# Attention, MLP and routed experts on one core: hidden values kept in PSUM, maxima scaled on ScalarE, sums applied to the attention's output in two of four batches

## Chip, cores and metric

One core of one Trainium2 chip. The metric is the time of one execution in microseconds of the device. Engines: PE is TensorE (matmul), PEld its weight loads, DVE is VectorE, ACT is ScalarE, POOL is GpSimd, SP is SyncE, which issues most DMAs here.

## What is computed

Attention with two kinds of masks, an MLP with a PReLU, and a layer of eight experts of which each token uses one.

```
scores = q @ k.T / 8;  masked (heads 0-3: local, 32 back; heads 4-7: every 32nd)
attn   = exp(scores - max);  attn /= sum + 1e-9;  a = attn @ v     # 4 batches, 8 heads, 576 x 64
h = x @ w_in;  g = max(h, 0) + alpha * min(h, 0);  y = g @ w_out   # 2304 x 512, 2048 hidden
e = argmax(y @ w_gate);  out = gate * sigmoid * relu(y @ w1[e]) @ w2[e]   # 8 experts, 1024 hidden
```

## The kernel before

The program fixes the order of the instructions on each engine by hand; an engine runs its instructions in that order, and waits where an input or a buffer is not there yet.

The attention works on groups: a pair of heads of one batch and one or two tiles of query rows (96, 126 or 72 rows), so two or four score tiles. There are 24 groups in batches 0 and 1 (`b < PE_MASK`) and 24 in batches 2 and 3. A group passes through a chain of steps, a step later each time: scores on TensorE (L218 to L240), in batches 0 and 1 with the mask added by a matmul; maxima on VectorE (L252), and L255 that multiplies them by the scale; the exponentials with their sums on ScalarE (L280); the sums' reciprocal on VectorE (L294, L295) and the normalization of the probabilities on GpSimd (L296; group 9 on VectorE); two steps after the scores their transposition on TensorE (L312) and a copy out of PSUM on ScalarE (L314); three steps after them the product with the values on TensorE (L327), a rounded copy on ScalarE (L366) and what rounding left out on VectorE (L371). The two parts are the input of the MLP.

The MLP runs over 6 blocks of 384 tokens with 16 iterations of 128 hidden values each, n = 0 to 95. Iteration n issues the first product of n + 2 (`mlp_in`, L438 to L440) into one of two PSUM banks, its activation (`mlp_act`: two relus on ScalarE, L447 and L448, and their sum on VectorE, L449), its split into a rounded part (L458 on ScalarE) and a rest (L460: GpSimd in block 0, VectorE later), and the second product of n (`mlp_out`, L473 to L475). Block 0 also carries a step of the attention in nearly every iteration, and up to iteration 11 the decoding of one weight: float64 words become two float32r parts by L401 (ScalarE), L405, L406 and L412 (VectorE), L420 (ScalarE) and L421 (GpSimd).

The order in an iteration: exponentials and reciprocals of the last step's group; first product of n + 2; values and output (L366, L371) of the group three steps back; the activation of n + 2; L420 and L421 of weight n + 4; scores and maxima of this step's group; L405, L406 and L412 of weight n + 5; second product of n with the transposition in between; L401 of weight n + 6; the split of n + 2.

Before block 0 stands a prologue of 13 steps for groups 0 to 9 with the decoding of the first weights. Steps 10 to 22 run in iterations 1 to 13 of block 0, eight more steps in each of the blocks 1 and 2, the others in block 3. The routing and the experts follow.

Of the kernel before, what the change touches and what calls it, by code (L numbers as in the profile page):

```python
# [15 lines left out]
P = 128  # L16
# [11 lines left out]
BLK = 384  # L28
# [21 lines left out]
# Splits ahead of the turn of the tokens of the place after next, by the kinds of three places in a row.  # L50
# [3 lines left out]
# When the parts of the second plan, its lists and its indices come: (place, position).  # L54
WHEN = ((0, 7), (1, 1), (1, 1), (1, 4), (1, 6))
OHP = 12
# Groups that VectorE normalizes, and groups whose scores come after matmuls that keep TensorE awake.
NRV = (9,)
FS = {2: 2}
# Parts of the first two products of the MLP that run between the last steps of the first attention.  # L60
# [23 lines left out]
def attention_prelu_mlp_routed_experts_kernel(  # L84
# [40 lines left out]
    with tc.manual_schedule():  # L125
# [20 lines left out]
        # A visit is a pair of heads of a batch and the groups of its rows that are worked on in turn.  # L146
# [56 lines left out]
        sc_t, p_t, pt_t, px_t = {}, {}, {}, {}  # L203
# [38 lines left out]
        def att_max(gi):  # L242
# [7 lines left out]
            if b < PE_MASK:  # L250
# [4 lines left out]
                nc.vector.tensor_scalar_mul(nm[:r, :nu], nm[:r, :nu], SCALE)  # L255
# [15 lines left out]
        def att_exp(gi):  # L271
# [5 lines left out]
            sm = apool.tile([P, 4], F32, tag="sm", name="sm", bufs=3)  # L277
# [12 lines left out]
        def att_norm(gi):  # L290
# [4 lines left out]
            nc.vector.reciprocal(sm[:r, :nu], sm[:r, :nu])  # L295
            (nc.vector if gi in NRV else nc.gpsimd).tensor_tensor(  # L296
# [6 lines left out]
        def att_transpose(gi, tag):  # L303
            local, js, r, kk = shape_of(gi)
            nu = 2 * len(js)
            pt = p_t.pop(gi)[0]
# [10 lines left out]
        def att_values(gi, tag):  # L317
# [7 lines left out]
            for ii, j in enumerate(js):  # L325
                for h2 in range(2):
                    mm(  # L327
                        px[h2 * D : (h2 + 1) * D, ii * P : ii * P + r],
                        v[:kk, j, h2, :],
                        ptt[:kk, h2 * len(js) + ii, :r],  # L330
                        start=True,
                        stop=True,
                    )
            px_t[gi] = px

        def att_store(gi):
            b, pr, g = groups[gi]
            local, js, r, kk = shape_of(gi)
            pxu = px_t.pop(gi).rearrange("p (u k) -> p u k", k=P)
            moves = []  # L340
# [51 lines left out]
        # A weight comes as a float64, two words; it leaves as the sum of two float32r.  # L392
# [49 lines left out]
        def mlp_act(n):  # L442
            c = n % NC1
            ph = h_t.pop(n)
            a = xpool.tile([P, BLK], F32, tag="a", name="a", bufs=2)
            bn = xpool.tile([P, BLK], F32, tag="bn", name="bn", bufs=1)
            nc.scalar.activation(out=a, in_=ph[:, :BLK], func=AF.Relu)  # L447
            nc.scalar.activation(out=bn, in_=ph[:, :BLK], func=AF.Relu, scale=-1.0)  # L448
            nc.vector.scalar_tensor_tensor(  # L449
                out=a, in0=bn, scalar=nalpha[:, c : c + 1], in1=a, op0=ALU.mult, op1=ALU.add  # L450
            )
            h_t[n] = a

        def mlp_split(n):
            a = h_t.pop(n)
            gh = xpool.tile([P, BLK], F32R, tag="gh", name="gh", bufs=3)
            gl = xpool.tile([P, BLK], F32R, tag="gl", name="gl", bufs=2)
            nc.scalar.activation(out=gh, in_=a, func=AF.Copy)  # L458
            eng = nc.gpsimd if n < NC1 else nc.vector
            eng.tensor_tensor(out=gl, in0=a, in1=gh.bitcast(F32), op=ALU.subtract)  # L460
# [97 lines left out]
        def route_parts(blk):  # L558
            """One-hot choice, weight and place in its expert's list of each token of a block."""
# [76 lines left out]
        def plan_parts(early):  # L636
            """A column is a list of up to 128 tokens of one expert, a place's tokens one or two columns. The
            first EARLY columns hold pairs of full lists of the tokens before the last block. The others
            of each expert come in pairs from C_P on, a last odd one from C_S on; but a last one of FEW
            tokens or less has its column from C_Q on."""  # L640
# [851 lines left out]
```

## Time and profile before

| | |
|---|---|
| median of 3 runs | 835.61 us (835.5 to 835.98) |
| span of the profiled execution | 831.9 us |
| busy PE, PEld | 784.2 us (94%), 659.6 us (79%) |
| busy DVE, ACT, POOL | 478.4 us (58%), 427.3 us (51%), 244.5 us (29%) |
| mean granted TensorE clock | 0.980 of full speed |

The span runs from the first to the last instruction; what starts and ends the execution around it is in the run's time only. Busy time of VectorE and GpSimd holds the time in which an issued operation waits for the other engine. In a timeline a row is an instruction with its start, its duration and its engine; starts of consecutive instructions of one engine can lie closer than their durations.

### The profile page before, as it was taken

The page shows a single profiled execution, that of the slowest core. Times are in us where ns is not written, and L with a number is a line of the kernel's source. Part 1 is how long each engine was busy: PE and PEld are TensorE (multiplying, and loading weights), DVE is VectorE, ACT ScalarE, POOL GpSimd, SP SyncE. Part 2 cuts the span into 40 slices and gives each one's busy share as a digit, 9 for nine tenths or more (in the row PEclk, how much of TensorE's full clock was granted, in tenths as well). Part 3 has the DMA queues.
Part 4 walks back from the last instruction along what each step waited for, and adds up shares of the span by engine and source line. Part 5 has one row for each costly group of instructions (what it writes and reads, how often), then busy time and mean ns, then how long its engine had stood idle before and what let it go on. Part 6 is the DMA issues. An engine that isn't in the chain of part 4 may idle for free. (4 is left out here: it accounts for less than half of the span.)

```text
span 831.9 us, 13663 instructions
## 1 busy us (share of the span) xinstructions
PE 784.2 (94%) x5032; PEld 659.6 (79%) x5035; DVE 478.4 (58%) x988; ACT 427.3 (51%) x1033; POOL 244.5 (29%) x168
## 2 busy tenths in 40 slices
PE   7687878999999999999999999999989998999995
PEld 4475766788888888888799898889878876878884
DVE  5989999345534554556333424757595447854422
ACT  6756665454455444665433333356534656655542
POOL 2756655200000000110000000032483354546422
PEclk9998999999999999999999999999999999999998
DMA  9716511101200121011000100362224577777421
GB/s 342 298 43 244 190 33 45 44 22 56 84 18 1 47 86 64 1 45 39 1 1 1 39 0 1 149 244 103 77 77 147 194 258 255 285 288 267 161 90 38
DMA packets 22621, 91.04 MB, mean 109 GB/s; under 512 B 3082, under 2 KB 7312, under 8 KB 15376
## 3 DMA queue, kind: packets, MB, share of 16 engines
q1 hardware_dynamic: 18816, 78.52, 26.6%
q0 software_dynamic: 3728, 11.55, 3.9%
q8 instruction: 41, 0.67, 0.3%
q14 instruction: 36, 0.29, 0.1%
HBM read 105.78 MB, written 9.97 MB: 139 GB/s over the span
## 5 line engine op out<-in xcount | busy, mean ns | idle before, releaser
L449 DVE SCALAR_TENSOR_TENSOR a<-bn,nalpha,a 128x384 f32<-128x384 f32 x96 | 73.2, 763 | 116.4 <-ACT bn L448 116.0
L438 PE MATMUL h<-xh,w 128*128 128x384 f32 x384 | 130.4, 340 | 0.4 <-ACT bn L448 0.4
L440 PE MATMUL h<-xh,w 128*128 128x384 f32 x384 | 129.9, 338 | 0.0
L439 PE MATMUL h<-xl,w 128*128 128x384 f32 x384 | 129.7, 338 | 0.0
L296 POOL TENSOR_TENSOR p<-p,sm 96x512 f32<-96x512 f32 (+2 forms) x47 | 48.7, 1036 | 267.6 <-DVE sm L295 255.3
L473 PE MATMUL acc<-w,gh 128*128 128x512 f32 x288 | 126.9, 441 | 0.0
L888 DVE TENSOR_TENSOR wx<-raw,wx 128x1024 fp32r<-128x1024 f32 x72 | 97.1, 1392 | 46.6 <-ACT wx L886 46.3
L475 PE MATMUL acc<-w,gl 128*128 128x512 f32 x288 | 115.8, 402 | 0.3 <-POOL gl L460 0.3
L474 PE MATMUL acc<-w,gh 128*128 128x512 f32 x288 | 115.6, 401 | 0.0
L886 ACT ACTIVATE wx<-raw 128x1024 fp32r<-128x1024 f32 x96 | 94.6, 1056 | 7.3 <-DMA raw<-in_wexp_dram 7.3
L447 ACT ACTIVATE a<-h 128x384 f32<-128x384 f32 x96 | 47.1, 491 | 99.7 <-PE h L440 99.6
L1042 PE MATMUL acc<-wx,hh 128*128 128x512 f32 x304 | 96.8, 400 | 0.0
L888 POOL TENSOR_TENSOR wx<-raw,wx 128x1024 fp32r<-128x1024 f32 x24 | 63.1, 2629 | 89.1 <-ACT wx L886 88.9
L438 PEld LDWEIGHTS h<-xh,w 128*128 128x128 f32 x384 | 73.1, 190 | 5.1 <-ACT bn L448 0.8
L439 PEld LDWEIGHTS h<-xl,w 128*128 128x128 f32 x384 | 72.9, 190 | 4.0
L440 PEld LDWEIGHTS h<-xh,w 128*128 128x128 f32 x384 | 72.6, 189 | 0.0
L895 POOL DMA_INDIRECT xg<-rows,idx_in x23 | 29.4, 1278 | 145.7 <-DVE a L449 139.3
L458 ACT ACTIVATE gh<-a 128x384 fp32r<-128x384 f32 x96 | 49.9, 520 | 42.6 <-DVE a L449 42.5
L475 PEld LDWEIGHTS acc<-w,gl 128*128 128x128 f32 x288 | 55.5, 193 | 14.2 <-POOL gl L460 0.8
L1042 PEld LDWEIGHTS acc<-wx,hh 128*128 128x128 f32 x304 | 56.5, 191 | 11.1
L473 PEld LDWEIGHTS acc<-w,gh 128*128 128x128 f32 x288 | 55.2, 192 | 11.1 <-issue 0.8
L460 DVE TENSOR_TENSOR gl<-a,gh 128x384 fp32r<-128x384 f32 x80 | 44.5, 556 | 28.7 <-ACT gh L458 16.6
(260 smaller groups left out, 1573.7 us busy)
## 6 DMA issues: line engine op xcount, KB each, us to landing
raw<-in_wexp_dram SPq DMA_DIRECT2D x64, 1024.0 KB
raw<-in_wp_dram SPq DMA_DIRECT2D x16, 1024.0 KB
qk<-in_qkv_dram SPq DMA_DIRECT2D x10, 576.0 KB
rows<-stage SPq DMA_DIRECT2D x15, 256.5 KB
v<-in_qkv_dram SPq DMA_DIRECT2D x8, 320.0 KB
qk<-in_qkv_dram SPq DMA_DIRECT2D x4, 384.0 KB
v<-in_qkv_dram SPq DMA_DIRECT2D x6, 256.0 KB
qk<-in_qkv_dram SPq DMA_DIRECT2D x4, 224.0 KB
```

The source lines that it names most:

```text
L296: (nc.vector if gi in NRV else nc.gpsimd).tensor_tensor(out=pt[:r, :nu, :kk], in0=pt[:r, :nu, :kk], in1=sm[:r, :nu].unsqueeze(2).to_broadc ...
L438: mm(ph[:, :BLK], w_in(c, 0, k), xh[:, k, :], start=(k == 0), stop=False)
L439: mm(ph[:, :BLK], w_in(c, 0, k), xl[:, k, :], start=False, stop=False)
L440: mm(ph[:, :BLK], w_in(c, 1, k), xh[:, k, :], start=False, stop=(k == KD - 1))
L449: nc.vector.scalar_tensor_tensor(out=a, in0=bn, scalar=nalpha[:, c : c + 1], in1=a, op0=ALU.mult, op1=ALU.add)
L458: nc.scalar.activation(out=gh, in_=a, func=AF.Copy)
L473: mm(o, gh[:, t], w_out(c, 0), start=(c == 0), stop=False)
L474: mm(o, gh[:, t], w_out(c, 1), start=False, stop=False)
L475: mm(o, gl[:, t], w_out(c, 0), start=False, stop=(c == NC1 - 1))
L886: nc.scalar.activation(out=w[:, :1024], in_=raw, func=AF.Copy)
L888: eng.tensor_tensor(out=w[:, 1024:], in0=raw, in1=w[:, :1024].bitcast(F32), op=ALU.subtract)
L1042: mm(po[i], h[:, h0 : h0 + P], wk[:, w0 : w0 + 512], start=st, stop=sp)
```

## The change

The activation works in PSUM: the second relu writes back into the bank of the first product, L449's sum goes there too, and the split reads it from there; the rest L460 is computed on VectorE in all blocks. In batches 0 and 1 the maxima are scaled by ScalarE, ahead of the exponentials; the probabilities are not normalized, but TensorE spreads the reciprocal sums over 64 partitions (a product with the identity) beside the values, ScalarE copies them to SBUF, and VectorE multiplies the output by them in PSUM. `sm` has four buffers in place of three; no group is normalized on VectorE. Comments are left out of the new text.

```diff
-NRV = (9,)
+NRV = ()
...
@@ att_max
-                nc.vector.tensor_scalar_mul(nm[:r, :nu], nm[:r, :nu], SCALE)
@@ att_exp
-            sm = apool.tile([P, 4], F32, tag="sm", name="sm", bufs=3)
+            sm = apool.tile([P, 4], F32, tag="sm", name="sm", bufs=4)
+            if b < PE_MASK:
+                nc.scalar.activation(out=nm[:r, : 2 * nj], in_=nm[:r, : 2 * nj], func=AF.Copy, scale=SCALE)
@@ att_norm
+            if groups[gi][0] < PE_MASK:
+                return
             (nc.vector if gi in NRV else nc.gpsimd).tensor_tensor(
@@ att_transpose
-            pt = p_t.pop(gi)[0]
+            pt, rs_t[gi] = p_t.pop(gi)
@@ att_values
+            rs = rs_t.pop(gi)
+            if b < PE_MASK:
+
+                for ii in range(len(js)):
+                    for h2 in range(2):
+                        u = h2 * len(js) + ii
+                        mm(
+                            px[h2 * D : (h2 + 1) * D, 256 + ii * P : 256 + ii * P + r],
+                            rs[:r, u : u + 1].to_broadcast([r, D]),
+                            ident[:r, :r],
+                            start=True,
+                            stop=True,
+                        )
@@ att_store
+            if b < PE_MASK:
+                v = pxu[:, : len(js), :r]
+                rb = apool.tile([P, 2, P], F32, tag="rb", name="rb", bufs=1)[:, : len(js), :r]
+                nc.scalar.activation(out=rb, in_=pxu[:, 2 : 2 + len(js), :r], func=AF.Copy)
+                nc.vector.tensor_tensor(out=v, in0=v, in1=rb, op=ALU.mult)
@@ mlp_act
+            v = ph[:, :BLK]
             a = xpool.tile([P, BLK], F32, tag="a", name="a", bufs=2)
-            bn = xpool.tile([P, BLK], F32, tag="bn", name="bn", bufs=1)
-            nc.scalar.activation(out=a, in_=ph[:, :BLK], func=AF.Relu)
-            nc.scalar.activation(out=bn, in_=ph[:, :BLK], func=AF.Relu, scale=-1.0)
+            nc.scalar.activation(out=a, in_=v, func=AF.Relu)
+            nc.scalar.activation(out=v, in_=v, func=AF.Relu, scale=-1.0)
             nc.vector.scalar_tensor_tensor(
-                out=a, in0=bn, scalar=nalpha[:, c : c + 1], in1=a, op0=ALU.mult, op1=ALU.add
+                out=v, in0=v, scalar=nalpha[:, c : c + 1], in1=a, op0=ALU.mult, op1=ALU.add
             )
-            h_t[n] = a
+            h_t[n] = v
@@ mlp_split
-            nc.scalar.activation(out=gh, in_=a, func=AF.Copy)
-            eng = nc.gpsimd if n < NC1 else nc.vector
-            eng.tensor_tensor(out=gl, in0=a, in1=gh.bitcast(F32), op=ALU.subtract)
+            nc.scalar.activation(out=gh, in_=v, func=AF.Copy)
+            nc.vector.tensor_tensor(out=gl, in0=v, in1=gh.bitcast(F32), op=ALU.subtract)
```

## Rows read from the trace of the kernel before

**Rows 1.** Windows: span, each engine's busy us (instructions), granted clock, DMA share, GB/s

```profile
80.00:90.00 10.00, 7.70 (x42) 6.16 (x40) 9.86 (x11) 5.52 (x15) 8.01 (x5) 0.83 0.76 301
...
150.00:160.00 10.00, 10.00 (x67) 8.60 (x65) 3.19 (x11) 4.28 (x15) 3.06 (x3) 1.00 0.20 66
```

**Rows 2.** Single lines of code, whole span: duration ns minimum/median/maximum, first and last start

```profile
L449 DVE SCALAR_TENSOR_TENSOR a<-bn,nalpha,a x96: 600/619/3815, 50.2 to 557.6; 128x384 f32<-128x384 f32 x96
...
L371 DVE TENSOR_TENSOR xl<-T,xh x56: 168/323/358, 84.1 to 413.7; 128x192 fp32r<-128x192 f32 x20, 128x84 fp32r<-128x84 f32 x12, 128x168 fp32r<-128x168 f32 x12, 128x24 fp32r<-128x24 f32 x6
...
L460 DVE TENSOR_TENSOR gl<-a,gh x80: 546/558/560, 162.3 to 558.9; 128x384 fp32r<-128x384 f32 x80
...
L421 POOL TENSOR_TENSOR w<-stage,w x16: 2342/2582/3347, 23.5 to 142.2; 128x1024 fp32r<-128x1024 f32 x16
```

**Rows 3.** Timeline of VectorE, one iteration of block 0: start us, duration us

```profile
91.80 0.16 DVE L294 TENSOR_SCALAR sm<-sm 72x2 f32<-72x2 f32 x1
...
92.47 0.67 DVE L449 SCALAR_TENSOR_TENSOR a<-bn,nalpha,a 128x384 f32<-128x384 f32 x1
93.06 0.41 DVE L252 TENSOR_REDUCE nm<-sl_bank 96x2 f32<-96x256 f32 x1
...
93.83 1.76 DVE L255 TENSOR_SCALAR nm<-nm 96x4 f32<-96x4 f32 x1
95.51 0.68 DVE L405 TENSOR_SCALAR stage<-stage 128x1024 int32<-128x1024 int32 x1
96.22 1.92 DVE L406 SCALAR_TENSOR_TENSOR stage<-raw,stage 128x1024 int32<-128x1024 int32 x1
98.17 1.23 DVE L412 SCALAR_TENSOR_TENSOR stage<-raw,stage 128x1024 int32<-128x1024 int32 x1
99.31 0.16 DVE L294 TENSOR_SCALAR sm<-sm 96x4 f32<-96x4 f32 x1
```

**Rows 4.** Timeline of GpSimd, the same iteration

```profile
93.16 2.41 POOL L421 TENSOR_TENSOR w<-stage,w 128x1024 fp32r<-128x1024 f32 x1 [0.44 <-ACT w L420]
95.52 1.53 POOL L460 TENSOR_TENSOR gl<-a,gh 128x384 fp32r<-128x384 f32 x1
```

**Rows 5.** Timeline of VectorE: marks of iterations 1, 4 and 11

```profile
60.73 0.60 DVE L449 SCALAR_TENSOR_TENSOR a<-bn,nalpha,a 128x384 f32<-128x384 f32 x1
...
83.85 0.16 DVE L294 TENSOR_SCALAR sm<-sm 126x4 f32<-126x4 f32 x1
...
140.69 0.16 DVE L294 TENSOR_SCALAR sm<-sm 96x4 f32<-96x4 f32 x1
```

**Rows 6.** Groups by line, GpSimd, 20:145 us: count, busy us, mean ns, idle before

```profile
L421 POOL TENSOR_TENSOR w<-stage,w 128x1024 fp32r<-128x1024 f32 x16 | 42.8, 2674 | 8.7 <-ACT w L420 8.7
L296 POOL TENSOR_TENSOR p<-p,sm 126x504 f32<-126x504 f32 (+2 forms) x16 | 18.5, 1158 | 35.2 <-DVE sm L295 35.2
L460 POOL TENSOR_TENSOR gl<-a,gh 128x384 fp32r<-128x384 f32 x13 | 17.9, 1375 | 5.6 <-ACT gh L458 5.4
```

**Rows 7.** Timeline of TensorE: the eight value passes of one group, merged

```profile
96.73 0.65 PE L327 MATMUL T<-ptt,v 126*64 126x126 f32 x8
```

**Rows 8.** Timeline of ScalarE, one iteration of block 0

```profile
97.43 0.46 ACT L366 ACTIVATE xh<-T 128x84 fp32r<-128x84 f32 x2 [0.31 <-PE T L327]
97.76 0.49 ACT L447 ACTIVATE a<-h 128x384 f32<-128x384 f32 x1
98.12 0.51 ACT L448 ACTIVATE bn<-h 128x384 f32<-128x384 f32 x1
99.43 1.06 ACT L420 ACTIVATE w<-stage 128x1024 fp32r<-128x1024 f32 x1 [0.79 <-DVE stage L412]
```

**Rows 9.** Timeline of ScalarE in the prologue, in brackets the idle time before

```profile
12.96 0.34 ACT L280 ACTIVATE p<-sl_bank,nm 96x128 f32<-96x128 f32 x1
...
30.02 0.59 ACT L314 ACTIVATE ptt<-acc 126x504 f32<-126x504 f32 x1 [2.21 <-PE acc L312]
...
37.94 0.31 ACT L280 ACTIVATE p<-h,nm 72x72 f32<-72x72 f32 x1
```

More of the change, by code (lines that the diff above doesn't have):

```diff
@@ L201, in xt @@
             return xh_t[blk], xl_t[blk]
-        sc_t, p_t, pt_t, px_t = {}, {}, {}, {}
+        sc_t, p_t, pt_t, px_t, rs_t = {}, {}, {}, {}, {}
         def masks(gi):
@@ L444, in mlp_act @@
             ph = h_t.pop(n)
+            v = ph[:, :BLK]
             a = xpool.tile([P, BLK], F32, tag="a", name="a", bufs=2)
-            bn = xpool.tile([P, BLK], F32, tag="bn", name="bn", bufs=1)
-            nc.scalar.activation(out=a, in_=ph[:, :BLK], func=AF.Relu)
-            nc.scalar.activation(out=bn, in_=ph[:, :BLK], func=AF.Relu, scale=-1.0)
+            nc.scalar.activation(out=a, in_=v, func=AF.Relu)
+            nc.scalar.activation(out=v, in_=v, func=AF.Relu, scale=-1.0)
             nc.vector.scalar_tensor_tensor(
-                out=a, in0=bn, scalar=nalpha[:, c : c + 1], in1=a, op0=ALU.mult, op1=ALU.add
+                out=v, in0=v, scalar=nalpha[:, c : c + 1], in1=a, op0=ALU.mult, op1=ALU.add
             )
-            h_t[n] = a
+            h_t[n] = v
         def mlp_split(n):
-            a = h_t.pop(n)
+            v = h_t.pop(n)
             gh = xpool.tile([P, BLK], F32R, tag="gh", name="gh", bufs=3)
             gl = xpool.tile([P, BLK], F32R, tag="gl", name="gl", bufs=2)
-            nc.scalar.activation(out=gh, in_=a, func=AF.Copy)
-            eng = nc.gpsimd if n < NC1 else nc.vector
-            eng.tensor_tensor(out=gl, in0=a, in1=gh.bitcast(F32), op=ALU.subtract)
+            nc.scalar.activation(out=gh, in_=v, func=AF.Copy)
+            nc.vector.tensor_tensor(out=gl, in0=v, in1=gh.bitcast(F32), op=ALU.subtract)
             g_t[n] = (gh, gl)
```

## Prediction

> **What bounds the kernel now.** I read the page's busy shares first, then the table of windows, then the timelines of one iteration engine by engine. From 160 us on TensorE has no gap and is the bound: already in 150:160 it is busy 10.00 of 10 us, VectorE 3.19 [rows 1]. Before that it is not: in 80:90 TensorE is busy 7.70 us at a granted clock of 0.83, VectorE 9.86 and GpSimd 8.01 [rows 1]. So the time that this change can move lies in the first 150 us: the prologue (attention of groups 0 to 9, five weights decoded) and block 0 of the MLP (16 iterations, in the first eleven of which a further weight is decoded on ScalarE, VectorE and GpSimd).
>
> VectorE's 9.86 us are not all work. L449 takes between 0.60 and 3.82 us [rows 2], and in one iteration the scaling of four maxima, L255, took 1.76 us: issued at 93.83, it ended at 95.59, as GpSimd's L421, begun at 93.16, ended at 95.57 [rows 3, 4]. L406 at 96.22 is held in the same way by L460, which ends at 97.05 [rows 3, 4]. Operations whose inputs are all in SBUF wait for a GpSimd pass in flight, or GpSimd waits for them. L371, with one input in PSUM, was never over 0.358 us in 56 runs [rows 2]: such operations don't wait.
>
> VectorE's own work of one iteration, from start to start: L294, L295 and L371 0.67, L449 0.59, two L252 0.77, L255 0.09, L405 0.71, L406 1.23 (as the free L412), L412 1.14: 5.2 us [rows 3]. From iteration 4 to 11 it took 140.69 - 83.85 = 56.84 us for seven, 8.12 each [rows 5]; some 2.9 us of each are waits for GpSimd.
>
> **The change, part by part.**
>
> *Taken away.* L255 leaves VectorE (0.09 us of work, the wait of whatever came next). GpSimd loses the normalization L296 of 24 groups and the sixteen L460: 18.5 and 17.9 us of its 79.2 in 20:145 [rows 6]. The weight pass L421 stays, 2.34 us when nothing holds it [rows 2], and is all that VectorE can still collide with. L449 reads one input from PSUM and no longer waits; by L371 I keep its free 0.60.
>
> The Trainium skill ("Perfetto Trace Analysis", Optimizing Scalar/DVE Operations) gives VectorE about 60 ns of access time on SBUF and 125 on PSUM, ScalarE the reverse, 93 and 51. This speaks against both passes in PSUM; by it two VectorE passes and two ScalarE passes would be, as an estimate, about 0.05 us dearer per iteration together, +0.4 us in all. The rows don't show it: the PSUM operation of 192 columns took 0.323, the SBUF one of 384 columns 0.558 [rows 2].
>
> *Added.* VectorE gets the sixteen L460 (0.50 us from start to start) and for each group of batches 0 and 1 a product in PSUM, about 0.33 to 0.42 us by L371's size. ScalarE gets the scaling of the maxima (not in this trace; between 0 and the 0.32 us of a pass over 192 columns; I take 0.23, near the upper end, since short passes are nearly all fixed cost) and the copy of the sums, 0.33 us. TensorE gets eight passes per group of four scores like those of L327, whose eight came 0.054 us apart: 0.32 to 0.43 us [rows 7].
>
> *Moved, and this is where I think the gain goes.* The order of a ScalarE iteration becomes: exponentials, copy of the sums, L366, two relus, L420. L366 now waits for VectorE's product, and the product stands in VectorE's queue behind the previous iteration's L412, L460, L294 and L295. Before, L366, the relus and L449's inputs were done ahead: relus at 97.76 and 98.12, while L420 waited until 99.43 for L412 alone [rows 8]. Now the relus, L420 and thereby L421 wait for VectorE, and VectorE's next decoding waits for L421.
>
> Iterations 4 to 10, from one L412's end to the next: L460 0.50, L294 and L295 0.30 (two short passes), product 0.42 with hand-over, L366 to relu 0.33, relu to relu 0.36, to L420 0.38, L420 1.06 [rows 8], hand-over 0.10, L421 2.34 [rows 2]; then L405, which was ready 0.3 us after L421 began (L449 and two L252 take about as long as L420), 0.55 after release, L406 1.23, L412 1.14. That is 8.7; for the smaller groups 8.45 to 8.6, mean 8.65. Against 8.12: +0.53 x 7 = +3.8 us. Bounds: 7.5 (if L421 is hidden to the same share as now) to 9.2 (if the copy of the sums is late as well): -4.3 to +7.6.
>
> Iterations 1 to 3 have no output to scale yet, so L420 starts at L412's end: L420 1.06, hand-over 0.13, L421 2.34, L405 0.55, L406 1.23, L412 1.14 = 6.5 each. From 60.73 to 83.85 they took 23.1 [rows 5]; 19.5 after: -3.6 us.
>
> Prologue: from the exponentials at 12.96 to those at 37.94 are seven steps [rows 9]. Each gets 0.23 + 0.33 + some 0.40 of waiting for the product, 0.97 us, in ScalarE's queue: 6.8 us. ScalarE had six gaps of 4.6 us in all there, the longest 2.21 [rows 9], and one transposition starts 0.3 us sooner since it needs no GpSimd pass: +1.9. The first two tiles of hidden values now stay in their banks until L460 has read them, and TensorE's third waits, about 0.7; shorter waits of L294 at the prologue's end give about 0.9 back. I take +1.7 at 60.73; bounds 0 and +3.5.
>
> Tail of block 0 (iterations 11 to 15): L449's longest wait goes, 3.8 us less its free 0.6 [rows 2], but TensorE, without a gap soon after [rows 1] and with the sums' passes added, is next: I take a good third of it, -1.2 (0 to -2). Block 1: four groups of batch 1 are left, where TensorE has no gap: four times 0.32 of passes and 0.1 of waiting for the bank behind the longer copy-product-copy-rest: +1.8 (+1.3 to +3). Later blocks and the experts: nothing; the hidden bank is released 3 us before its next use.
>
> Sum: +1.7 - 3.6 + 3.8 - 1.2 + 1.8 = +2.5 us. The profiled span is 831.9, the median of the runs 835.6; the 3.7 around the span stay. **838.1 us.**
>
> **Rivals.**
>
> A, faster: the holds fall in proportion. If L421 doesn't come in step with VectorE's queue, VectorE loses what GpSimd's remaining share, 42.8 of 79.2 [rows 6], makes of 2.9: 1.6, and its own work is 5.2 - 0.2 + 0.5 + 0.4 = 5.9. Iterations 4 to 10 then take 7.5, -4.4 us, and the prologue comes out even: -3.6 - 4.4 - 1.2 + 1.8 = -7.4, **828.2 us**. For it: VectorE is the busiest engine of the stretch and loses the most. Against: the order of ScalarE's queue puts L421 behind the product every time. It decides if VectorE has over 1 us of work without a wait left when L421 begins; I count 0.3. The Trainium skill's advice to work first on the engine with the highest occupancy ("Perfetto Trace Analysis", Identifying the Most-Contended Engine) would have this come true; the rows agree that VectorE is that engine, but a third of its occupancy is waiting.
>
> B, no change: the chain holds, but ScalarE's gaps swallow the prologue's additions, so +2.5 - 1.7 = +0.8: **836.4**, or less.
>
> C, slower still: TensorE idles about 2 us in every one of iterations 4 to 10; gaps of this kind go with the 0.83 of [rows 1]. If its clock stays low through the first product, the sums come after VectorE is ready for them, some 0.7 us each: +4.9, **843 us**.
>
> **How the numbers follow.** Forecast (836.9 to 840.5) 0.45, A 0.26, B 0.17, C 0.12. A measurement of this kernel tells about 0.2%, 1.7 us, from no change: faster is below 833.9, slower above 837.3. Faster: A and the lower edge of B, 0.29. Same: B and the forecast's lower edge, 0.24. Slower: the rest, 0.47. The range runs to the centre of A and of C, 827.5 to 843.
>
> **What would show it.** Right: L366 waiting for VectorE's product in block 0; L405 stretched beyond 0.68 us, up to 2.5; L449 never over 0.65; starts of L294 8.5 to 8.8 us apart from iteration 4 to 10, 6.5 in 1 to 3; ScalarE's gaps in the prologue filled; spans from 160 us on unchanged but for about 0.4 us per group in block 1. Wrong: L421 beginning before the relus, L405 at 0.68, or L449 still stretched.

## Result

| | before | changed | change |
|---|---|---|---|
| median of the runs | 835.56 us (832.13 to 835.98, 4 runs) | 842.34 us (841.78 to 844.66, 4 runs) | ratio 1.0099 [1.007, 1.0127] |
| span of the profiled execution | 831.9 us | 840.4 us | +8.5 us |
| busy VectorE / GpSimd in 80:90 | 9.86 / 8.01 us [rows 1] | 9.05 / 3.74 us | -0.81 / -4.27 us |

The kernel is 6.8 us slower; the forecast was 2.5 us slower. The medians differ by 6.8 us and the two spans by 8.5; the rest is in the experts of the one execution shown before (last part of this section).

The window of the changed kernel that answers to the first of [rows 1] (columns as there):

```profile
80.00:90.00 10.00, 7.04 (x45) 5.44 (x45) 9.05 (x13) 6.96 (x24) 3.74 (x2) 0.86 0.77 296
```

GpSimd has lost more than half of its busy time, and VectorE is still 90% busy. Busy time fell on both, and block 0 did not get shorter.

Lines answering to [rows 2] and those that are new (duration ns minimum/median/maximum, first and last start). L449 is now L470, L460 L480, L405 L426, L406 L427, L412 L433, L420 L441, L421 L442, L366 L387, L371 L392, and L294 and L295 are L295 and L296:

```profile
L470 DVE SCALAR_TENSOR_TENSOR h<-h,nalpha,a x96: 591/626/629, 51.8 to 563.1; 128x384 f32<-128x384 f32 x96
...
L480 DVE TENSOR_TENSOR gl<-h,gh x96: 547/558/560, 53.0 to 564.3; 128x384 fp32r<-128x384 f32 x96
...
L426 DVE TENSOR_SCALAR stage<-stage x16: 678/1483/2873, 15.2 to 139.8; 128x1024 int32<-128x1024 int32 x16
...
L442 POOL TENSOR_TENSOR w<-stage,w x16: 2344/2496/3427, 23.4 to 148.1; 128x1024 fp32r<-128x1024 f32 x16
...
L278 ACT ACTIVATE nm<-nm x24: 188/204/230, 7.0 to 185.4; 96x4 f32<-96x4 f32 x12, 126x4 f32<-126x4 f32 x8, 72x2 f32<-72x2 f32 x4
...
L359 ACT ACTIVATE rb<-T x14: 231/330/382, 82.1 to 207.9; 128x192 f32<-128x192 f32 x8, 128x252 f32<-128x252 f32 x4, 128x72 f32<-128x72 f32 x2
...
L360 DVE TENSOR_TENSOR T<-T,rb x14: 211/367/429, 85.0 to 208.3; 128x192 f32<-128x192 f32 x8, 128x252 f32<-128x252 f32 x4, 128x72 f32<-128x72 f32 x2
```

L470 reads PSUM and never waits for GpSimd: its longest is 0.63 us where L449 had 3.82 [rows 2]. The wait has gone to L426, up to 2.87 us; as L405 its 16 runs took no more than 0.68. In two of iterations 4 to 10 L426 began first and ran its 0.68 us, and the instruction behind it, L427, was held instead: 3.28 and 3.29 us where it takes 1.22. The new instructions cost what the forecast gave them: L278 0.20 us (0.23), L359 0.33 (0.33), L360 0.37 (0.33 to 0.42).

The marks of iterations 1, 4 and 11 on VectorE, as in [rows 5]:

```profile
64.50 0.62 DVE L470 SCALAR_TENSOR_TENSOR h<-h,nalpha,a 128x384 f32<-128x384 f32 x1
...
84.70 0.16 DVE L295 TENSOR_SCALAR sm<-sm 126x4 f32<-126x4 f32 x1
...
145.50 0.15 DVE L295 TENSOR_SCALAR sm<-sm 96x4 f32<-96x4 f32 x1
```

Set against [rows 5] they give the first three lines of this table; the others are the starts of L449 and L470 for the tiles n = 18 (169.42 and 173.24), n = 27 (219.51 and 225.75) and n = 93 (547.95 and 554.71), taken from the same timelines.

| stretch | forecast | profile, changed less before |
|---|---|---|
| start to iteration 1 (handover) | +1.7 | +3.77 |
| iterations 1 to 3 | -3.6 | -2.92 |
| iterations 4 to 10 | +3.8 | +3.96 |
| tail of block 0 (to n = 18) | -1.2 | -0.99 |
| block 1 (n = 18 to 27) | +1.8 | +2.42 |
| later blocks (to n = 93) | 0 | +0.52 |
| sum | +2.5 | +6.76 |
| router and experts | 0 | +1.72 |

Up to n = 93 the profiles differ by 6.76 us, as the medians do (6.78). Behind it the changed kernel has one stretch of half clock on TensorE (window; start:end, length, PE, PEld, DVE, ACT and POOL busy, granted clock, DMA share, GB/s):

```profile
585.00:590.00 5.00, 5.00 (x31) 5.00 (x32) 2.95 (x19) 0.44 (x3) 1.43 (x3) 0.66 0.66 226
```

In the execution shown before, the same window had 1.00. From n = 93 to the end of the span, the kernel before took 284.0 us, the changed one 285.7, and ten of the variants below, none of which touches this part, between 284.2 and 287.2. The 1.7 us lie inside that scatter, and I do not count them to the change.

### The profile page after: what moved, and what is told of

It is laid out like the page before. It is cut to its first block, busy times and chain, and to the rows that moved or that the text cites. A ratio compares the mean times of both kernels' runs of the same rounds, so it can differ in the third digit from the quotient of the medians.

```text
span 840.4 us, 13990 instructions
## 1 busy us (share of the span) xinstructions
PE 796.7 (95%) x5211; PEld 670.3 (80%) x5211; DVE 468.3 (56%) x1003; ACT 433.4 (52%) x1081; POOL 195.9 (23%) x129
## 5 line engine op out<-in xcount | busy, mean ns | idle before, releaser
L459 PE MATMUL h<-xh,w 128*128 128x384 f32 x384 | 132.0, 344 | 4.1 <-DVE gl L480 2.7
L460 PE MATMUL h<-xl,w 128*128 128x384 f32 x384 | 130.9, 341 | 0.0
L470 DVE SCALAR_TENSOR_TENSOR h<-h,nalpha,a 128x384 f32<-128x384 f32 x96 | 60.0, 625 | 118.2 <-ACT h L469 118.1
L495 PE MATMUL acc<-w,gl 128*128 128x512 f32 x288 | 115.6, 401 | 0.0
L468 ACT ACTIVATE a<-h 128x384 f32<-128x384 f32 x96 | 47.2, 491 | 104.4 <-PE h L461 104.4
L459 PEld LDWEIGHTS h<-xh,w 128*128 128x128 f32 x384 | 74.0, 193 | 10.1 <-DVE gl L480 4.3
L460 PEld LDWEIGHTS h<-xl,w 128*128 128x128 f32 x384 | 73.7, 192 | 4.2
L299 POOL TENSOR_TENSOR p<-p,sm 96x512 f32<-96x512 f32 (+2 forms) x24 | 22.4, 931 | 234.5 <-DVE sm L296 222.3
L461 PEld LDWEIGHTS h<-xh,w 128*128 128x128 f32 x384 | 73.5, 191 | 0.0
L480 DVE TENSOR_TENSOR gl<-h,gh 128x384 fp32r<-128x384 f32 x96 | 53.3, 555 | 30.6 <-PE acc L495 15.3
L442 POOL TENSOR_TENSOR w<-stage,w 128x1024 fp32r<-128x1024 f32 x16 | 42.3, 2644 | 107.8 <-ACT w L441 49.2
L495 PEld LDWEIGHTS acc<-w,gl 128*128 128x128 f32 x288 | 55.1, 191 | 13.4
L479 ACT ACTIVATE gh<-h 128x384 fp32r<-128x384 f32 x96 | 46.8, 488 | 34.1 <-DVE h L470 34.0
```

Of the source, the lines that this page charges most:

```text
L459: mm(ph[:, :BLK], w_in(c, 0, k), xh[:, k, :], start=(k == 0), stop=False)
L460: mm(ph[:, :BLK], w_in(c, 0, k), xl[:, k, :], start=False, stop=False)
L461: mm(ph[:, :BLK], w_in(c, 1, k), xh[:, k, :], start=False, stop=(k == KD - 1))
L468: nc.scalar.activation(out=a, in_=v, func=AF.Relu)
L470: nc.vector.scalar_tensor_tensor(out=v, in0=v, scalar=nalpha[:, c : c + 1], in1=a, op0=ALU.mult, op1=ALU.add)
L480: nc.vector.tensor_tensor(out=gl, in0=v, in1=gh.bitcast(F32), op=ALU.subtract)
```

## The order of an iteration, as it came

ScalarE of one iteration (timeline: start, duration, in brackets the idle time before and what ended it):

```profile
117.02 0.33 ACT L359 ACTIVATE rb<-T 128x192 f32<-128x192 f32 x1 [0.25 <-PE T L343]
119.99 0.33 ACT L387 ACTIVATE xh<-T 128x192 fp32r<-128x192 f32 x1 [2.64 <-DVE T L360]
120.22 0.48 ACT L468 ACTIVATE a<-h 128x384 f32<-128x384 f32 x1
120.59 0.50 ACT L469 ACTIVATE h<-h 128x384 f32<-128x384 f32 x1
121.00 1.05 ACT L441 ACTIVATE w<-stage 128x1024 fp32r<-128x1024 f32 x1
```

VectorE of the same and the iteration before:

```profile
113.63 2.79 DVE L426 TENSOR_SCALAR stage<-stage 128x1024 int32<-128x1024 int32 x1
116.46 1.23 DVE L427 SCALAR_TENSOR_TENSOR stage<-raw,stage 128x1024 int32<-128x1024 int32 x1
117.72 1.23 DVE L433 SCALAR_TENSOR_TENSOR stage<-raw,stage 128x1024 int32<-128x1024 int32 x1
118.86 0.55 DVE L480 TENSOR_TENSOR gl<-h,gh 128x384 fp32r<-128x384 f32 x1
...
119.62 0.34 DVE L360 TENSOR_TENSOR T<-T,rb 128x192 f32<-128x192 f32 x1
```

GpSimd:

```profile
113.45 2.42 POOL L442 TENSOR_TENSOR w<-stage,w 128x1024 fp32r<-128x1024 f32 x1 [6.10 <-ACT w L441]
122.13 2.72 POOL L442 TENSOR_TENSOR w<-stage,w 128x1024 fp32r<-128x1024 f32 x1 [6.25 <-ACT w L441]
```

ScalarE has the copy of the sums done at 117.35 and stands still for 2.64 us until the product L360, which is queued behind L433 and L480. Only then come the output, the two relus and L441. L441 starts 2.0 us after L433 ended (118.95); in [rows 8] it started 0.03 us after L412's end. GpSimd's pass follows and holds L426. One turn, from L442 to L442, took 8.68 us.

The Trainium skill ("SBUF — State Buffer", SBUF: two separate sides) says that VectorE and GpSimd share a pair of ports; of a GpSimd operation and a VectorE operation that needs the pair (one with two inputs in SBUF, or in a mode that uses both pairs of VectorE) the one that begins first has it for its whole length, and the other stands still. The trace agrees: L442 began 0.18 us ahead of L426 at 113.45, ran its 2.42, and L426 ended 0.55 us after it. Where L426 began first, at 121.94, it took 0.68 us, and L442, begun at 122.13, took 2.72.

## Experiments

Marks used below are the starts of L449 or L470 (the PReLU of tile n) on VectorE. n = 3 is the mark of iteration 1; from n = 6 to n = 13 are iterations 4 to 10. The variants ran in three sets, with the kernel before beside each: its median was 836.45 us beside experiments 1 to 4, 835.59 beside 5 to 8 and 834.6 beside 9 to 11. The ratios below are against the one beside; between sets, a difference of 2 us or less is read from the marks and not from the medians.

| kernel | n = 0 | n = 3 | n = 6 | n = 13 | per iteration, 4 to 10 | median |
|---|---|---|---|---|---|---|
| before | 50.16 | 60.73 | 84.38 | 141.18 | 8.11 | 835.56 |
| changed | 51.78 | 64.50 | 86.50 | 147.12 | 8.66 | 842.34 |
| MLP part alone | 50.69 | 63.91 | 86.05 | 136.48 | 7.20 | 830.39 |
| attention part alone | 52.13 | 62.70 | 86.23 | 149.45 | 9.03 | 847.3 |
| changed, other order | 52.30 | 65.52 | 86.02 | 140.56 | 7.79 | 837.58 |
| changed, early banks | 52.68 | 62.95 | 84.96 | 145.59 | 8.66 | 841.77 |
| before without L255 | 49.06 | 59.60 | 82.73 | 139.22 | 8.07 | 833.58 |
| changed, no product | 47.83 | 61.06 | 81.81 | 132.37 | 7.22 | (not comparable) |
| MLP part, early banks | 50.90 | 61.05 | 83.19 | 134.81 | 7.37 | 826.23 |
| the same, no L255, late normalization | 49.49 | 59.63 | 81.80 | 134.55 | 7.54 | 827.14 |
| changed, pass on VectorE | 54.45 | 67.16 | 87.41 | 144.56 | 8.16 | 839.55 |
| MLP part, early banks, pass on VectorE | 51.33 | 60.97 | 81.85 | 129.64 | 6.83 | 822.6 |
| the same, no L255 | 50.19 | 59.91 | 80.20 | 126.79 | 6.66 | 821.43 |

### 1. The MLP part alone

The kernel before, with the changed activation and split and nothing else:

```diff
-            nc.scalar.activation(out=bn, in_=ph[:, :BLK], func=AF.Relu, scale=-1.0)
+            nc.scalar.activation(out=v, in_=v, func=AF.Relu, scale=-1.0)
...
-            eng = nc.gpsimd if n < NC1 else nc.vector
-            eng.tensor_tensor(out=gl, in0=a, in1=gh.bitcast(F32), op=ALU.subtract)
+            nc.vector.tensor_tensor(out=gl, in0=v, in1=gh.bitcast(F32), op=ALU.subtract)
```

> The kernel before with the MLP's part of the change alone (activation and split in PSUM, the rest L460 on VectorE for all n); the attention as before. Theory S (what the change loses in block 0 is lost by the order on ScalarE: relus, L420 and so the GpSimd pass L421 stand behind the attention's new product): there is no product here, so L420 starts at L412's end; L296 then L421 hold GpSimd until 4.2 us after L412's end, L255 waits for that, then L405, L406, L412 3.1: 7.3 us per iteration in place of 8.1, some -9 us over iterations 1 to 11, and +2 to +3 at the start of block 0, since the third first product waits for a bank: 827 to 832. Rival T (the added VectorE work is what costs, L460 above all): +0.5 us in each of 12 iterations and the start: 840 to 845.

Measured: 830.39 us, ratio 0.9924 [0.9903, 0.9945], inside theory S's range. Iterations 4 to 10 take 7.20 us each, 6.4 us less in all. The handover alone, though, costs +3.2 us at n = 3, and TensorE's timeline shows where:

```profile
52.47 0.69 PE L438 MATMUL h<-xh,w 128*128 128x384 f32 x1 [3.69 <-DVE gl L459]
52.96 0.52 PE L439 MATMUL h<-xl,w 128*128 128x384 f32 x1
53.28 0.52 PE L440 MATMUL h<-xh,w 128*128 128x384 f32 x1
```

The third first product waits 3.69 us until the split of the first tile has read its bank (L459 is the rest of the split here), and then its matmuls start 0.32 us apart, where 0.17 is usual at full clock.

### 2. The attention part alone

The changed kernel with the activation and the split of the kernel before (its copy of the sums uses the buffer of the negative parts, for space):

```diff
-            nc.scalar.activation(out=v, in_=v, func=AF.Relu, scale=-1.0)
+            nc.scalar.activation(out=bn, in_=ph[:, :BLK], func=AF.Relu, scale=-1.0)
...
-            nc.vector.tensor_tensor(out=gl, in0=v, in1=gh.bitcast(F32), op=ALU.subtract)
+            eng = nc.gpsimd if n < NC1 else nc.vector
+            eng.tensor_tensor(out=gl, in0=a, in1=gh.bitcast(F32), op=ALU.subtract)
```

> The changed kernel with the MLP's activation and split as in the kernel before (hidden values to SBUF, L460 on GpSimd in block 0); the attention's part of the change stays. Theory S: the chain through the product stays and L460 on GpSimd comes back as a second hold: 8.2 to 9.1 us per iteration in 4 to 10 (8.69 in the changed kernel, 8.12 before), no wait for banks at the start: 838 to 844. Rival T: with L460 off VectorE and L255 and L296 gone VectorE has less to do than in either kernel: under 835.

Measured: 847.3 us, ratio 1.013 [1.0113, 1.0147]: slower by 10.9, 3 us beyond theory S's upper end and far from T. Iterations 4 to 10 take 9.03 us each (+6.4 us in all). At n = 0 and at n = 3 it stands at +1.97. This is the prologue by itself, for which the forecast had +1.9, less the 0.9 that was to come back at its end.

The two parts together make +4.8 us by their medians (-6.1 and +10.9), and the whole change made +6.8. In iterations 4 to 10, -6.4 and +6.4 would cancel, and the whole change has +3.8: of what the MLP part gains alone, 2.6 us are left once the chain through the product is there.

### 3. The order on ScalarE

The changed kernel, in iterations 0 to 11 with the relus and the weight pass ahead of the attention's product and output:

```diff
                 att_values(s - LV, "T")
+            if n + DEC < NC1:
+                mlp_act(n + 2)
+                decode(n + DEC, 4)
+            if on(s - LV):
                 att_store(s - LV)
             att_back(s)
...
```

> The changed kernel, but in the iterations that decode a weight (0 to 11) the activation (two relus, L470) and L441 with L442 come ahead of the copy of the sums, the product and L387; the same instructions otherwise. Theory S: L441 starts at L433's end again, L442 ends 3.5 us after it, the product and the two passes behind it run under L442: 6.6 to 7.0 us per iteration in 4 to 10 in place of 8.69, that is -12 to -15 us: 827 to 831. Rival T (VectorE's own work and holds in proportion): the same work and the same holds, so 841 to 843. Half-way (835): the later product makes TensorE wait for its bank.

Measured: 837.58 us (10 runs), ratio 1.0014 [0.9999, 1.0029]: 4.8 us faster than the changed kernel, neither S's 11 to 15 nor T's nothing. In the middle it does what S said. ScalarE of one iteration:

```profile
110.44 1.04 ACT L441 ACTIVATE w<-stage 128x1024 fp32r<-128x1024 f32 x1
111.38 0.22 ACT L359 ACTIVATE rb<-T 128x72 f32<-128x72 f32 x1
```

L441 now goes ahead of the copy, L442 runs from 111.56 to 113.92, and L426, from 113.11, takes 1.37 rather than 2.79 us. Six of the seven iterations 4 to 10 take 7.1 to 7.9 us. The seventh takes 9.05, because what was moved back holds bank T longer. TensorE there:

```profile
87.87 1.10 PE L315 MATMUL T<-cst,p 126*126 126x126 f32 x4 [3.26 <-DVE xl L392]
...
89.62 0.63 PE L495 MATMUL acc<-w,gl 128*128 128x512 f32 x1
90.05 0.63 PE L493 MATMUL acc<-w,gh 128*128 128x512 f32 x1
```

The transposition waits 3.26 us for the rest of the output, and half clock follows: two matmuls of 512 columns start 0.43 us apart, where 0.23 is usual. From n = 13 to 16 it loses another 2.5 us against the changed kernel (20.15 against 17.67 us), where the old order comes back; part of this is only that the mark L470 stood earlier in an iteration before that. So the order is the cause of the long iterations. Part of the gain from turning it is lost at the bank that the product occupies, and part in waits for ScalarE, which S had left out: in 84:142 VectorE waits 11.3 us in all for the relus, the copy of the sums and L387 (5.6 in the changed kernel).

### 4. Early banks

The changed kernel; the negative parts of tiles 0 and 1 go to SBUF, so that their banks are free at the second relu:

```diff
...
+            w = v
+            if n < 2:
+                w = xpool.tile([P, BLK], F32, tag="bn", name="bn", bufs=1)
-            nc.scalar.activation(out=v, in_=v, func=AF.Relu, scale=-1.0)
+            nc.scalar.activation(out=w, in_=v, func=AF.Relu, scale=-1.0)
+            v = a if n < 2 else v
...
```

> The changed kernel, but for n = 0 and 1 the activation goes to SBUF as in the kernel before, so that their banks are free after the second relu. Theory: at the start of block 0 the third first product no longer waits 2.58 us for L480 and does not run at half clock behind that wait; L470 of n = 2 comes 2 to 2.5 us earlier: 839.5 to 841. Rival: VectorE is the bound there and the wait only moves: 842.

Measured: 841.77 us (840.43 to 842.49), ratio 1.0061 [1.0041, 1.0081]; by the median the rival's 842 is nearer. Against the kernel before beside it, it is 5.3 us slower, where the changed kernel was 6.8. The profile shows the same effect: n = 3 comes at 62.95 instead of 64.50, and the 1.5 us are kept to n = 93 (553.21 against 554.71). n = 0 came 0.9 us later than in the changed kernel, for which the buffer that L359 here shares with the negative parts is a possible cause; I didn't separate it. From n = 0 to n = 3 the gain is 2.45 us. The half clock, which was expected to go, stayed: the matmuls of the third product start 0.32 us apart from 52.28 to 55.16. The experts of the profiled execution took 1.4 us longer. Experiment 7 asks the same question with less beside it.

### 5. Who waits for GpSimd

The kernel before without L255; the maxima of batches 0 and 1 are subtracted unscaled:

```diff
-                nc.vector.tensor_scalar_mul(nm[:r, :nu], nm[:r, :nu], SCALE)
```

> The kernel before without L255: the maxima of batches 0 and 1 are subtracted unscaled (the exponent's shift is larger by a factor that the division by the sums takes out again). Theory S (VectorE and GpSimd exclude each other on SBUF, and whichever VectorE instruction comes next pays): the wait of some 1.7 us moves from L255 to the decoding's first step, which then takes about 2.2 us rather than 0.68; iterations 4 to 10 stay at 7.9 to 8.2 us each, the time within 834 to 837. Rival T (the wait belonged to L255): each of the iterations 4 to 10 gets some 1.4 us shorter, time 825 to 828.

Measured: 833.58 us (10 runs), ratio 0.9981 [0.9963, 0.9998], 0.4 us below theory S's range. Iterations 4 to 10 take 8.07 us, as before (8.11), where T had some 1.4 us less. GpSimd's pass (L420 here) and the decoding's first step on VectorE (L404 here):

```profile
108.21 2.70 POOL L420 TENSOR_TENSOR w<-stage,w 128x1024 fp32r<-128x1024 f32 x1
...
109.25 2.21 DVE L404 TENSOR_SCALAR stage<-stage 128x1024 int32<-128x1024 int32 x1
```

L404 takes 2.21 us, just what theory S gave. The wait belongs to whatever stands next in VectorE's queue. What the removal did give lies for the most part outside these iterations: of 3.2 us up to n = 93, 1.1 lie in the prologue (n = 0 at 49.06 instead of 50.16) and 1.2 between n = 13 and n = 16, behind the last of them. The experts of this execution took 1.7 us longer, so the medians show 2.0.

### 6. Without the product

The changed kernel without L359 and L360, so the output of batches 0 and 1 isn't divided by the sums. The tokens then go to other experts, and the time of the whole (967.8 us) says nothing; only the marks of the first blocks are read.

```diff
-            if b < PE_MASK:
+            if False:
                 v = pxu[:, : len(js), :r]
```

> The changed kernel without the copy of the sums (L359) and the product (L360): the attention's output of batches 0 and 1 is left undivided by the sums, which is the part of the computation that it leaves out. Theory S (ScalarE's relus and weight pass stand behind the product): without it L387 and the relus go ahead as in the kernel before, the weight pass starts when L433 ends, and iterations 4 to 10 take 6.5 to 6.8 us each rather than 8.66, -13 to -15 us there, and block 1 gives back some 0.2 us per group: 826 to 830. Rival T (only the instructions' own times count, 0.34 on VectorE and 0.33 on ScalarE): 8.0 to 8.3 us each, 837 to 840.

Measured: iterations 4 to 10 take 7.22 us instead of 8.66, -10.1 us. This is nearer to S (6.5 to 6.8) than to T (8.0 to 8.3), as the two instructions' own 0.67 us are less than half of the 1.44 us that go. ScalarE:

```profile
109.25 0.33 ACT L387 ACTIVATE xh<-T 128x192 fp32r<-128x192 f32 x1 [0.82 <-PE T L343]
...
110.25 1.05 ACT L441 ACTIVATE w<-stage 128x1024 fp32r<-128x1024 f32 x1
```

L441 starts 0.36 us after L433's end (109.89) rather than 2.0. Two of the iterations take 6.54 and 6.69 us, as S said. The first takes 8.16: L387 waits 2.82 us there for TensorE's sums, and VectorE 0.98 us for L387, which S had left out. What makes the other four 7.0 to 7.6 us long isn't worked out. n = 0 comes at 47.83, 2.3 us before that of the kernel before: in the prologue the change without copy and product is worth -2.3 us, and copy and product add 3.95. In block 1 (n = 18 to 27) this kernel takes 1.42 us more than the kernel before, and the changed one 2.42.

### 7. The MLP part with early banks

The first experiment's kernel with the edit of the fourth.

> The MLP part alone (830.4), and the negative parts of its first two tiles go to SBUF, so that their banks come free at the second relu rather than at the splitting. Theory (the banks of the first two tiles hold up TensorE's third first product, and the half clock after that wait makes it dearer): the wait of 3.7 us falls below 0.6, the third tile's L449 starts 2.5 to 3.2 us sooner (57.7 to about 54.8), iteration 1's at 60.7 to 61.3, and the time is 827 to 828.5. Rival (TensorE then waits as long for something else, the first two tiles' splits or a weight): third tile no more than 0.8 us sooner, 829.5 to 830.5.

Measured: 826.23 us (825.99 to 829.5), ratio 0.9902 [0.9864, 0.994], 0.8 us under the expected range; against the kernel before beside each, 3.3 us faster than experiment 1. VectorE's third tile, and TensorE's window of the handover:

```profile
54.83 0.63 DVE L453 SCALAR_TENSOR_TENSOR h<-h,nalpha,a 128x384 f32<-128x384 f32 x1 [0.20 <-ACT h L451]
```

```profile
45.00:65.00 20.00, 15.74 (x83) 12.50 (x82) 18.24 (x23) 11.97 (x24) 8.16 (x3) 1.00 0.29 84
```

The tile comes at 54.83 (54.8 expected, 57.69 without the edit), the granted clock of 45:65 is 1.00 where the first experiment had 0.83, and n = 3 stands at 61.05, 0.3 us from the kernel before and 2.9 ahead of experiment 1. The bank is the cause of the handover's cost. Of the 2.9 us, 1.6 are left at n = 93: iterations 4 to 10 take 7.37 us here and 7.20 there, the difference in iterations 8 and 9 (7.75 and 7.62 against 7.34 and 6.85), for which I have no cause.

### 8. The normalization behind the weight pass

The kernel of 7 without L255, with the normalization after the weight pass in GpSimd's queue:

```diff
-                nc.vector.tensor_scalar_mul(nm[:r, :nu], nm[:r, :nu], SCALE)
...
             if n + DEC < NC1:
                 decode(n + DEC, 4)
+            if on(s - 1):
+                att_scale(s - 1)
```

> The run with the MLP part alone and early banks, again without L255 (maxima unscaled, as in the other run), and with the normalization of the probabilities put behind the weight pass in GpSimd's queue in block 0. Theory S: the weight pass no longer stands behind a normalization of 0.4 to 1.0 us, so that an iteration is 0.1 + 1.06 + 2.4 + 0.6 + 1.23 + 1.23 = 6.6 us rather than 7.2, -4 us over seven, and the time is 822 to 825. Rival T (the normalization then excludes VectorE in the next stretch for as long as it did in this one): iterations stay at 7.1 to 7.3, 827 to 829.

Measured: 827.14 us, ratio 0.9905 [0.9872, 0.9938]. S fell; T's time is what came, and the iterations are even a little longer (7.54 us against 7.37). VectorE and GpSimd (L410 is the decoding's second step, L300 the normalization, which starts as the weight pass ends):

```profile
115.05 1.93 DVE L410 SCALAR_TENSOR_TENSOR stage<-raw,stage 128x1024 int32<-128x1024 int32 x1
```

```profile
114.42 1.48 POOL L300 TENSOR_TENSOR p<-p,sm 126x504 f32<-126x504 f32 x1
```

The normalization, moved out of the pass's way, holds L410 (1.93 us instead of 1.23). That L255 is gone too doesn't hide a gain: experiments 5 and 11 have 0.04 and 0.17 us per iteration for it. My sum had left GpSimd's second operation without anybody to pay for it.

### 9. The weight pass on VectorE

The changed kernel, with L442 on VectorE, so that GpSimd has nothing to do in iterations 4 to 10:

```diff
-            nc.gpsimd.tensor_tensor(out=w[:, 1024:], in0=t, in1=w[:, :1024].bitcast(F32), op=ALU.subtract)
+            nc.vector.tensor_tensor(out=w[:, 1024:], in0=t, in1=w[:, :1024].bitcast(F32), op=ALU.subtract)
```

> The changed kernel with the weight pass (L442) on VectorE, so that GpSimd has nothing left in iterations 4 to 10 to exclude VectorE with. Theory S (the chain through GpSimd's pass of 2.4 us sets the 8.66 us): L426 takes 0.68 us and L427 1.23 everywhere, and VectorE's own starts add up to L427 1.26, L433 1.14, L480 0.47, L295 and L296 0.29, L360 0.37 and 0.4 of waiting, L392 0.3 and 0.4, L470 0.53, L252 0.66, L426 0.71, the pass 1.1: 7.6 us per iteration, 833 to 836.5. Rival T (VectorE's added work is what costs; another 1.1 us on it adds to the 8.66): 9.5 to 9.8 us each, 847 to 851.

Measured: 839.55 us, ratio 1.0065 [1.0043, 1.0086], 2.8 us faster than the changed kernel: between the two theories, nearer to S.

```profile
L442 DVE TENSOR_TENSOR w<-stage,w x16: 1214/1226/1228, 22.9 to 145.5; 128x1024 fp32r<-128x1024 f32 x16
...
L426 DVE TENSOR_SCALAR stage<-stage x16: 677/682/689, 14.7 to 139.4; 128x1024 int32<-128x1024 int32 x16
```

No L426 is held any more, and iterations got shorter (8.16 from 8.66) although VectorE has 1.1 us more to do in each. By the marks it is 2.6 us ahead of the changed kernel at n = 93. My 7.6 was too low by the waits for ScalarE. VectorE's longest waits in 84:142 (engine, instruction, releaser; us in all, times, longest):

```profile
DVE xl L392 <- ACT xh L387: 3.2, 7, 0.5
DVE h L470 <- ACT h L469: 2.4, 7, 0.5
DVE w L442 <- ACT w L441: 2.3, 7, 0.3
```

Of these I had counted the first only, beside 0.4 us per iteration for L360, of which 0.5 us in all came. The prologue is 2.7 us longer here (n = 0 at 54.45), which I had not counted either.

### 10 and 11. A faster version

The kernel of 7 with the weight pass on VectorE, and the same without L255:

> The MLP part with early banks (826.2) and the weight pass on VectorE; GpSimd keeps the normalization. Theory S: VectorE's starts add up to 5.2 less nothing, plus L463's 0.47, plus 1.1 for the pass, less the hold of the pass: 6.3 us per iteration, up to 6.8 where the normalization of 1.03 us holds up what follows it; from 7.37, -4 to -7 us, 819.5 to 823. Rival T (VectorE at over 95% of these iterations is bound by work, not by holds): 7.4 to 8.4 us each, 826 to 833.

> The same without L255 (maxima of batches 0 and 1 subtracted unscaled). Theory S: the iterations don't change by more than 0.2 us each, since the wait for the normalization moves to the next instruction; the prologue gets 1.0 to 1.5 us shorter, as it did in the two runs without L255: 1 to 2 us less than with it. Rival T: the wait was L255's, 0.5 us and more per iteration go, 4 us less than with it.

Measured: 822.6 us, ratio 0.9859 [0.9829, 0.9889], and 821.43 us, ratio 0.9848 [0.9828, 0.9867]. Both beat both kernels; the second is 20.9 us under the changed one. Iterations 4 to 10 take 6.83 and 6.66 us; both times lie in theory S's ranges. Without L255 it is 1.2 us faster by the medians. The two profiles differ by 2.6 us at n = 93: 1.1 are there at n = 0 and n = 3, and iterations 4 to 10 give 0.17 us each, 1.2 in all; the experts of that execution took 2.6 us longer. Only the normalization is left to hold VectorE, and it now holds the pass itself (L421, 1.22 us when free):

```profile
L421 DVE TENSOR_TENSOR w<-stage,w x16: 1215/1528/1861, 22.4 to 130.2; 128x1024 fp32r<-128x1024 f32 x16
```

The Trainium skill's advice to work first on the engine with the highest occupancy ("Perfetto Trace Analysis", Identifying the Most-Contended Engine) would speak against giving VectorE another pass, as it is over 97% busy in these iterations in the kernel of 7 (49.76 of 51 us in 84:135). The measurement decides otherwise: some 1.9 us of each 7.4 were standing still for GpSimd (an estimate: the durations of VectorE's instructions less the shortest of each form; 0.3 us with the pass moved), and 1.2 us of work in place of a pass of 2.4 is cheaper.

## Why the prediction was right in direction and short in size

Up to n = 93 the profiles differ by 6.76 us where 2.5 were forecast. Of the 4.3 us between, 2.1 are the handover's, 0.7 those of iterations 1 to 3, 0.6 block 1's and 0.5 the later blocks'.

- *Iterations 4 to 10, +3.8 forecast, +3.96 measured.* Right, and for the reason given: 8.65 us each forecast, 60.80 / 7 = 8.69 by the marks. L387 waited 0.5 to 2.98 us for VectorE's product, L441 started 1.9 to 2.3 us after L433's end and L442 behind it, and L426 or L427 was held by it. By the durations less the shortest of each form, VectorE stood held for 3.6 us per iteration before and 2.2 after; what that gave went into its added work and into idle time, 0.2 us per iteration before and 0.9 after. Experiments 3 and 6 take the order or the product away and lose the long iterations; 9 takes the hold away. The product is in the chain as a wait, not as 0.34 us of work.
- *Iterations 1 to 3, -3.6 forecast, -2.92 measured.* Right in kind: 20.20 us for three instead of 19.5. The sum took L442 at its free 2.34; the one of iteration 1 ran 2.68 us, and from n = 3 to n = 4 it took 7.20.
- *Handover, +1.7 forecast, +3.77 measured: the step that failed.* It had three terms. The prologue, +1.9 forecast, had +2.5 at its last exponentials (40.41 instead of 37.94). That it came so near is in part luck: the seven steps took 3.4 us longer, since ScalarE waited 0.3 to 2.0 us for the product in each, 0.7 in the mean where 0.40 was forecast, and 0.9 us were gained ahead of the first of them, which the forecast didn't have. The 0.9 that was to come back at the prologue's end came, whatever gave it: +1.62 at n = 0. The third term, "TensorE's third waits, about 0.7", was wrong: from n = 0 to n = 3 the hold cost 3.77 - 1.62 = 2.15 us, and 2.65 in the MLP part alone (experiment 1). The changed kernel's TensorE:

```profile
53.56 0.69 PE L459 MATMUL h<-xh,w 128*128 128x384 f32 x1 [2.58 <-DVE gl L480]
54.05 0.52 PE L460 MATMUL h<-xl,w 128*128 128x384 f32 x1
54.37 0.52 PE L461 MATMUL h<-xh,w 128*128 128x384 f32 x1
...
56.57 0.34 PE L459 MATMUL h<-xh,w 128*128 128x384 f32 x1
56.74 0.34 PE L460 MATMUL h<-xl,w 128*128 128x384 f32 x1
```

  The wait was 2.58 us, not 0.7 (0.44 in the kernel before), and the matmuls behind it ran at half clock, 0.32 us apart until 56.29 instead of 0.17, some 1.4 us more. The half clock was there from 49.83 on, ahead of this wait, so it isn't shown that the wait brought it. VectorE at the first tile:

```profile
49.26 2.60 DVE L433 SCALAR_TENSOR_TENSOR stage<-raw,stage 128x1024 int32<-128x1024 int32 x1
51.78 0.61 DVE L470 SCALAR_TENSOR_TENSOR h<-h,nalpha,a 128x384 f32<-128x384 f32 x1
52.95 0.56 DVE L480 TENSOR_TENSOR gl<-h,gh 128x384 fp32r<-128x384 f32 x1 [0.56 <-ACT gh L479]
```

  I had priced the bank by the instruction that reads it last. What counts is the whole chain from the product over L468, L469, L470 and L479 to L480, and in it L470 stood behind L433, which took 2.60 us under GpSimd's weight pass instead of 1.21. From n = 0 to n = 3 experiments 4 and 7, in which the first two banks come free early, take 10.27 and 10.15 us, the kernel before 10.57: without the hold all of the 2.15 us are gone.
- *Tail, -1.2 forecast, -0.99 measured.* Right, and where it was said: L449's longest wait, 3.81 us, stood at n = 13, and from n = 13 to n = 14 it takes 6.46 us instead of 8.08.
- *Block 1, +1.8 forecast, +2.42 measured.* Mis-sized in one of its two parts. TensorE of one group in block 1:

```profile
188.12 0.55 PE L330 MATMUL T<-ptt,v 128*64 128x96 f32 x8
188.50 0.50 PE L343 MATMUL T<-cst,sm 96*64 96x96 f32 x8
188.93 0.35 PE L234 MATMUL sl_bank<-qk 64*96 64x128 f32 x1
...
190.12 0.39 PE L495 MATMUL acc<-w,gl 128*128 128x512 f32 x1
190.59 0.55 PE L315 MATMUL T<-cst,p 96*128 96x96 f32 x4
```

  The sums' passes put 0.81 us between the values and the scores where the kernel before has 0.48: +0.33, forecast 0.32. Experiment 6, which has them and no product, takes 1.42 / 4 = 0.36 us per group. The rest, (2.42 - 1.42) / 4 = 0.25 us, is the wait of L315 for bank T, for which I had 0.1: it starts 0.47 us after L495 here and 0.24 in experiment 6.
- *Later, nothing forecast, +0.52 to n = 93.* I can't name its place; it stands between n = 80 (+6.41) and n = 93 (+6.76) for the larger part. Experts: no change beyond the scatter.
- *"The 3.7 around the span stay".* Only 1.8 us lie around the span in the runs of both kernels that have both numbers, to 0.1 us (842.18 and 840.4, for one). So the profiled execution of the kernel before was some 1.9 us shorter than the median one; its experts, at 284.0 us, are the shortest of all the profiles. The sum was added to the median, so nothing followed from it.
- *Rivals.* A (828.2) needed L442 out of step with VectorE's queue; in iterations 4 to 10 it starts 0.2 us before or after L426 each time. The MLP part alone, which has no product, came near its time with 830.4. B fell with the prologue, +1.62 at n = 0 (+1.97 in the attention part alone). C's mechanism isn't what came: the granted clock of 83:146 was low (0.89, and 0.92 before), but in 84:142 VectorE never waited for the copy of the sums. That its 843 us are near is luck, by way of the handover above all.
- *Access times.* The Trainium skill ("Perfetto Trace Analysis", Optimizing Scalar/DVE Operations) would make a VectorE operation some 65 ns dearer in PSUM. L470 has a median of 626 ns against 619 for L449 and L480 558 against 558 for L460 [rows 2]: 7 and 0 ns. Leaving that estimate out of the sum was right.

## To carry to other kernels

Before an output is divided late instead of its inputs early, look at what stands behind the late step in the queue of the engine that takes it over: here a copy and a product of 0.33 and 0.34 us cost 1.4 us in each iteration, because a weight pass on a third engine stood behind them. Where two engines exclude each other, taking away an instruction that waits moved the wait to the next one (experiment 5); it went when the holder went (experiments 9 to 11). A buffer that is read later is priced by the whole chain up to the last reader, and by the clock of the matmul engine that waits for it.

## What had not been expected of the hardware

- The same pass over 128x1024 values takes 1.22 us on VectorE and 2.34 at the least on GpSimd, during which the next decoding step on VectorE stood still (L426 up to 2.87 us instead of 0.68). So VectorE was the cheaper place for it here, although it was the busiest engine (8.66 to 8.16 us, and 7.37 to 6.83, per iteration).
- TensorE's granted clock falls to the half, 1.2 GHz, around the waits of the handover, and the length of one wait doesn't tell when. With waits of 1.27 and 2.58 us the changed kernel has 0.83 in 45:65; in experiment 4, with 1.28 and 0.42 us, matmuls ran 0.32 us apart for 3.4 us all the same (0.91); in experiment 7, with waits of up to 1.3 us, it stayed at 1.00. A stretch of half clock also came at 585 to 589 us in the changed kernel, without idle time before it, behind 24 matmuls of 16 columns; the kernel before has the same matmuls and had none there.
